# A Fourier mixing and gated FFN kernel on one core: batch 0's x ahead of the weights, half tables read mirrored, half the sines inside the thirds, batch 1's first folds on VectorE

## The chip, the core and the metric

The kernel runs on one core of a Trainium2 chip. The core has TensorE (PE; its weight loads are listed apart as PEld), VectorE (DVE), ScalarE (ACT), GpSimd (POOL), SyncE (SP), whose only work here is to issue transfers, and 16 DMA engines. The metric is the device time of one execution in microseconds, lower is better; the median over several executions is quoted.

## The reference, cut to what matters

```python
X = np.fft.fft(np.fft.fft(x, axis=1), axis=2)      # x: (8, 3008, 256), float32
x = X.real.astype(np.float32).reshape(8 * 3008, 256)
gate = 1.0 / (1.0 + np.exp(-(x @ w_gate)))         # 256 x 1536
val = x @ w_val                                    # 256 x 1536
return (gate * val @ w_out).astype(np.float32)     # 1536 x 256
```

The three weights are handed over as 8-byte floats.

## The kernel before, in words

**Sequence transform.** The transform along the 3008 positions is a product with cosine and sine tables. Symmetry cuts it: rows s, S-s, M+s and M-s (M = 1504) are folded into sums and differences, so that 756 rows remain, held as 126 partitions times 6 slots q. Frequencies are split into even ones (block 0) and odd ones (block 1), and rows by their parity (slots with even and odd q, accumulated apart in banks `ev` and `od`). The table `st` (from `stab`) holds, for cosine and sine, slot q and both blocks, 753 columns: 377 for block 0 and 376 for block 1. `half` (L500 on) makes one group of sums: `sums(*qs)` issues one product per slot, `then` copies the `ev` bank out on ScalarE, and `places` (L535 to L541) writes sums and differences of `ev` and `od` on VectorE into rows of `pk` (cosine) or `qk` (sine), 128 features by 1505 frequencies. The feature transform is folded in the same way; its middle feature (number 128) gives one row, `er`, which is handled apart: `e0_sums`, `e0_copies`, `e0_row` and `e0_spread` for batch 0, `e_fold` (L600 to L604, on POOL) and `e_sums` for the other seven batches.

**Weights.** Gate and value weights come in twelve pieces of 256 x 256 (numbers 0 to 11), the output weights in six (12 to 17). `weight_load` transfers one (512 KB), `weight_parts` (L301, L302) takes it apart on ScalarE in two operations, `weight_join` (L313 to L316) puts float32 together in three VectorE operations and one POOL addition (L318). `merge` multiplies a gate or value piece with the feature table `dt` on TensorE, and `merged` (L349) copies the result to `G`, the combined matrix of feature transform and weights. Bias values `ge` for each block of 128 hidden features come out of row 0 of `G2`: for pieces 0 to 3 by one-column products (`ge_sums`, `ge_out`), for the others by small transfers (`ge_load`, L364).

**Main loop.** 8 batches times 6 chunks of 252 frequencies times 12 blocks of 128 hidden features make 576 passes. In pass i, `front_a(i)` and `front_b(i)` multiply `G` with `pk` and `qk`; `seed` (ScalarE, L664) puts the middle feature's row times `ge` into the bank beforehand, `part` (L675) saves the state between the two; `gate_a` and `gate_b` of pass i-1 make sigmoid and products (ScalarE L689, L703; VectorE L690, L702, L706), and POOL makes sums of blocks (L712) for `back`, the product with the output weights, in a form with fewer products (its weight forms are made by `forms` on POOL, L402 to L405). For the first chunk of batch 0, `rows_start` makes plain products instead.

**Order.** Each engine's order is written out by hand (the scheduler is set to manual for PE, ScalarE, VectorE, POOL and SP): an instruction that waits holds back all behind it on its engine. Lists (`mid`, `pre`, `use`, `side`) hang further work onto passes. In pass i the order is front_a(i), gate_a(i-1), part(i), seed(i+1), gate_b(i-1), listed work, back, front_b(i), work of `side[i]`. The next batch's x is folded in `side` work: `fold_ops` gives 24 operations for batch 1, in passes 24 to 55, and `table_odd` makes a smaller table on POOL in passes 56 to 60. SP issues transfers in program order; each waits until the eighth before it has landed.

**The start before.** SP issues pieces 0 to 7, then three thirds of batch 0's x (two slots each, 1 MB) with the cosine tables of the same slots, then the sine tables, between them pieces 8 and 9, then pieces 10 to 13. TensorE runs a warm-up and pieces 0 to 7; then, third by third, folds on VectorE (`third`, `feats`; L473 to L483) and cosine sums; then the sine sums third by third with front_a of passes 0 to 2 in between; then the loop.

## Time and profile before

| | |
|---|---|
| median of 3 runs | 1929.01 us (1926.16 to 1933.58) |
| profiled execution: time, span | 1929.26 us, 1927.4 us |
| TensorE busy, of the span | 1913.6 us, 99% |
| VectorE, ScalarE, POOL busy | 1406.6, 1343.7, 1557.4 us |
| granted TensorE clock | 1.000 |
| transferred | 97.89 MB, mean 51 GB/s |

The profile lists each engine's busy time, the same in slices and stretches, groups of instructions by source line (L135 is the helper `mm`, so TensorE's groups are told apart by their tiles: `ps` weight pieces, `pe` the middle feature's sums, `ev` and `od` sequence sums, `pf` front_a with `pk` and front_b with `qk`, `po` and `rows` the output), and the chain of waits: followed back from the end, at each step what released it. A timeline row gives start, length, engine, line, operation, tiles, shapes, count, and in brackets the engine's idle time before and what ended it. One logical float32 product shows as two records.

### The profile page before, as it was taken

The numbers are of one execution on the slowest core, as the hardware profiler recorded it, in microseconds if no ns is written. First come the engines' busy times: TensorE is split into PE (matmuls) and PEld (weight loads), VectorE is DVE, ScalarE is ACT, GpSimd is POOL, SyncE is SP. The second block draws the span as 40 slices with busy tenths as digits, with TensorE's granted clock in tenths as the row PEclk, the third lists the DMA queues.
The fourth block names the chain that finished last, engine by engine and source line by source line (L and its number), as shares of the span: only waits on it lengthen the run. The fifth ranks groups of instructions, "written<-read, shape, count | busy, mean of one in ns | idle before, by whom it ended". The sixth has DMA issues, their size and how long they took to land.

```text
span 1927.4 us, 34460 instructions
## 1 busy us (share of the span) xinstructions
PE 1913.6 (99%) x11260; PEld 1787.2 (93%) x11260; DVE 1406.6 (73%) x3210; ACT 1343.7 (70%) x3147; POOL 1557.4 (81%) x2806
## 2 busy tenths in 40 slices
PE   8999999999999999999999999999999999999999
PEld 5899999999999999999999999999999999999998
DVE  7747877787767776778777777777777777766776
ACT  5777767767777677776777767777677766777775
POOL 2399989978899688986888869888788886777775
PEclk9999999999999999999999999999999999999999
DMA  9351422211121201202112121111200100011111
GB/s 302 124 100 36 107 80 53 55 38 57 20 72 30 80 14 28 80 14 80 24 43 55 20 80 23 47 49 25 80 14 15 25 17 14 15 22 20 25 17 30
DMA packets 167403, 97.89 MB, mean 51 GB/s; under 512 B 128602, under 2 KB 157372, under 8 KB 165432
## 3 DMA queue, kind: packets, MB, share of 16 engines
q1 hardware_dynamic: 166670, 95.17, 20.5%
q8 instruction: 91, 1.49, 0.3%
q14 instruction: 88, 0.72, 0.1%
q10 hardware_dynamic: 522, 0.50, 0.1%
q0 software_dynamic: 32, 0.00, 0.0%
HBM read 70.40 MB, written 47.24 MB: 61 GB/s over the span
## 4 chain that ended last, share of the span: by engine, by line
PE 93%; POOL 3%; DMA 2%; ACT 0%; DVE 0%; issue 0%; ACTq 0%; SPq 0%; POOLq 0%
PE pf L135 49%; PE po L135 40%; PE ev L135 3%; POOL sf L712 2%; DMA st<-in_stab_dram 2%; PE rows L135 1%; PE od L135 1%; DMA x<-in_xf_dram 1%; PE row L135 0%; DMA raw<-in_moe_w_val_dram 0%; POOL x L452 0%; POOL x L431 0%; POOL x L436 0%; POOL x L433 0%; PE ps L135 0%
## 5 line engine op out<-in xcount | busy, mean ns | idle before, releaser
L712 POOL TENSOR_TENSOR sf<-h 128x168 f32<-128x168 f32 (+1 forms) x935 | 516.9, 572 | 224.8 <-DVE h L706 224.1
L712 POOL TENSOR_TENSOR sf<-h,sf 128x168 f32<-128x168 f32 (+1 forms) x1122 | 614.3, 568 | 49.2 <-DVE h L706 47.8
L135 PE MATMUL pf<-pk,G 128*128 128x252 f32 (+1 forms) x2304 | 582.9, 376 | 0.5 <-ACT pf L664 0.5
L135 PE MATMUL pf<-qk,G 128*128 128x252 f32 (+1 forms) x2304 | 581.8, 375 | 1.1 <-ACT ae L675 1.1
L664 ACT ACTIVATE pf<-ek,ge 128x252 f32<-128x252 f32 (+1 forms) x1152 | 542.6, 471 | 19.3 <-DVE h L706 0.5
L706 DVE TENSOR_TENSOR h<-pf,z 128x252 f32<-128x252 f32 (+1 forms) x576 | 241.6, 419 | 417.2 <-ACT pf L703 415.5
L135 PE MATMUL po<-sf,wf 128*128 128x168 f32 (+1 forms) x2992 | 516.6, 305 | 1.4 <-POOL sf L712 1.4
L675 ACT ACTIVATE ae<-pf 128x504 f32<-128x504 f32 (+1 forms) x576 | 339.8, 590 | 249.3 <-PE pf L135 247.8
L135 PEld LDWEIGHTS pf<-pk,G 128*128 128x128 f32 x2304 | 436.9, 190 | 53.4 <-issue 1.6
L135 PEld LDWEIGHTS po<-sf,wf 128*128 128x128 f32 x2992 | 460.6, 190 | 9.9 <-POOL sf L712 1.9
L135 PE MATMUL po<-h,wf 128*128 128x168 f32 (+1 forms) x2618 | 463.4, 305 | 0.0
L135 PEld LDWEIGHTS pf<-qk,G 128*128 128x128 f32 x2304 | 410.9, 190 | 27.3 <-ACT ae L675 1.5
L690 DVE TENSOR_TENSOR z<-ae,pf 128x504 f32<-128x504 f32 (+1 forms) x576 | 386.0, 670 | 65.3 <-ACT h L689 60.7
L135 PEld LDWEIGHTS po<-h,wf 128*128 128x128 f32 x2618 | 416.6, 190 | 16.2
L830 DVE TENSOR_TENSOR c<-c 128x168 f32<-128x168 f32 (+1 forms) x929 | 424.6, 465 | 3.4
L689 ACT ACTIVATE h<-pf 128x252 f32<-128x252 f32 (+1 forms) x576 | 218.9, 380 | 205.7 <-PE pf L135 195.4
L702 DVE TENSOR_TENSOR h<-h,pf 128x252 f32<-128x252 f32 (+1 forms) x576 | 233.5, 405 | 0.0
L703 ACT ACTIVATE pf<-z 128x252 f32<-128x252 f32 (+1 forms) x576 | 211.7, 368 | 24.4 <-DVE h L702 20.8
L712 POOL TENSOR_TENSOR sf<-sf 128x168 f32<-128x168 f32 (+1 forms) x187 | 103.5, 554 | 14.7
L712 POOL TENSOR_TENSOR sf<-sf,h 128x168 f32<-128x168 f32 (+1 forms) x187 | 110.6, 592 | 0.0
L743 ACT COPY c<-po 128x504 f32<-128x504 f32 (+1 forms) x141 | 80.1, 569 | 1.1 <-PE po L135 1.1
L839 DVE STREAM_TRANSPOSE os<-c 128x256 f32<-128x256 f32 x184 | 79.9, 435 | 0.0
(152 smaller groups left out, 906.5 us busy)
## 6 DMA issues: line engine op xcount, KB each, us to landing
x<-xr SPq DMA_DIRECT2D x14, 1536.0 KB
out_dram<-os SPq DMA_DIRECT2D x368, 56.0 KB
xr<-in_xf_dram SPq DMA_DIRECT2D x14, 768.0 KB
xr<-in_xf_dram SPq DMA_DIRECT2D x35, 256.0 KB
ek<-ed SPq DMA_DIRECT2D x39, 126.0 KB
out_dram<-os SPq DMA_DIRECT2D x284, 7.0 KB
st<-in_stab_dram SPq DMA_DIRECT2D x6, 658.9 KB
x<-in_xf_dram SPq DMA_DIRECT2D x3, 1024.0 KB
```

Of the source, the lines that this page charges most:

```text
L135: nc.tensor.matmul(o, l, r, start=start, stop=stop, skip_group_check=True)
L664: nc.scalar.activation(PF[i][:, g], EK[i // NFT], AF.Copy, scale=ge[:, g, f : f + 1])
L675: nc.scalar.activation(AP[i], PF[i], AF.Copy, scale=2.0)
L689: nc.scalar.activation(H[p][:, fh, 0:n], PF[i][:, 0], AF.Sigmoid)
L690: nc.vector.tensor_tensor(z[:, :, ::-1], AP.pop(i), PF[i], op=ALU.subtract)
L702: nc.vector.tensor_tensor(h[:, fh, 0:n], h[:, fh, 0:n], pf[:, 1], op=ALU.mult)
L703: nc.scalar.activation(pf[:, 0], z[:, 0], AF.Sigmoid)
L706: nc.vector.tensor_tensor(h[:, fh, n:], pf[:, 0], z[:, 1], op=ALU.mult)
L712: nc.gpsimd.tensor_tensor(block(p, dst), block(p, a), block(p, b), op=(ALU.subtract, ALU.add)[op])
L743: (nc.vector.tensor_copy if t == 1 or t == 3 and not last else nc.scalar.copy)(C[0][:, 3 * t * R : 3 * (t + 1) * R], PO[t][:, 0 : 3 * R])
L830: engine.tensor_tensor(t[:, dst * R : (dst + 1) * R], *v, op=(ALU.subtract, ALU.add)[op])
L839: nc.vector.transpose(os_[0][:, s, 0:nb, h, :], t[:, c0 : c0 + nb * TB])
```

## The change

It touches the start and the handling of batch 1.

- SP issues the three thirds of x first, each with its cosine and sine tables, then `dt`, then pieces 0 to 9 and 12; the others follow when their buffers are free. `dt` was issued by ScalarE before.
- Only half of each table's columns is loaded (377 of 753 per slot, one transfer of 126 rows; before, 112 rows and 14 rows). The other half of the frequencies is reached by reading the table backwards (`table_of(..., True)`) with cosine and sine exchanged for odd slots, against a copy of the folded x that has its signs set (`turned`, three ScalarE operations per third, with a per-partition sign from `signs`). So each product over 377 or 376 columns becomes two of 189 or 188.
- In the thirds, TensorE makes both cosine groups and the first sine group; the second sine group follows the last third in one go. After that come the weight pieces, and front_a of passes 0 to 2 between pieces 3 to 6. Warm-up grows from 12 to 16 products.
- Pieces 0 to 3 get their bias values by `ge_load` too; the one-column products are gone.
- The middle row of batch 0 (`e0_row`) is made on POOL. For the other batches `e_fold` gets three ScalarE copies with signs.
- Ahead of the loop pieces 0 to 8 are joined and 0 to 7 multiplied; pieces 9 to 12 are joined in passes 0 to 3.
- The first eight of batch 1's fold operations run on VectorE, two in each of passes 24 to 27 (before: POOL); the other sixteen stay on POOL in passes 28 to 55, and the odd table moves two passes ahead.

```diff
-        for rows in (slice(0, 112), slice(112, NP)):
-            nc.sync.dma_start(out=ST[0][rows, t, q], in_=stab[rows, t, q])
+        nc.sync.dma_start(out=ST[0][0:NP, t, q, 0 : HE + HO], in_=stab[:, t, q, HO : NE + HO])
...
+    def weight_parts(j, which=(0, 1)):
 
         if j in RAW:
             raw, ws = RAW[j], WS[j]
             lo, hi = raw[:, :, :, 0], raw[:, :, :, 1]
-            nc.scalar.activation(ws, hi.bitcast(F32), AF.Abs)
-            nc.scalar.activation(lo, lo.bitcast(U32), AF.Copy, scale=2.0 ** -29)
+            if 0 in which:
+                nc.scalar.activation(ws, hi.bitcast(F32), AF.Abs)
+            if 1 in which:
+                nc.scalar.activation(lo, lo.bitcast(U32), AF.Copy, scale=2.0 ** -29)
...
+    def signs():
+
+        at_ = sgn.bitcast(I32)
+        nc.gpsimd.iota(at_[:, 0:1], pattern=[[0, 1]], base=0, channel_multiplier=1)
+        nc.vector.tensor_scalar(out=at_[:, 1:2], in0=at_[:, 0:1], scalar1=31, scalar2=0x3F800000 - 2 ** 31,
+                                op0=ALU.logical_shift_left, op1=ALU.bitwise_xor)
+        nc.vector.tensor_scalar(out=at_[:, 0:1], in0=at_[:, 0:1], scalar1=31, scalar2=0x3F800000,
+                                op0=ALU.logical_shift_left, op1=ALU.bitwise_xor)
+
+    def sign(q, r=False):
+
+        i = (q // 2 % 2) ^ (r and q % 2 == 0)
+        return sgn[0:NP, i : i + 1]
...
-                ops += [lambda i=i, q=q: point(pool, i, i + 1, q) for q in qs]
-                ops.append(lambda i=i: first(pool, i, i + 1, slice(0, NQ)))
+                e = nc.vector if b == 1 else pool
+                ops += [lambda i=i, q=q, e=e: point(e, i, i + 1, q) for q in qs]
+                ops.append(lambda i=i, e=e: first(e, i, i + 1, slice(0, NQ)))
...
+            def turned(q):
+                copy = lambda to, of, s: nc.scalar.activation(to, of, AF.Copy, scale=s)
+                copy(XV[:, :, q, 0:HD], x4[:, 1::-1, q, 0:HD], sign(q.start))
+                for i in range(q.start, q.stop):
+                    copy(x4[:, 3:1:-1, i, HD:D], x4[:, 3:1:-1, i, 0:HD], sign(i, True))
+            XR_[0] = [(XV[:, i], x4[:, 3 - i, :, HD:D]) for i in range(2)]
             for q in qs:
-                ops += [lambda q=q: third(q), lambda q=q: feats(q)]
+                ops += [lambda q=q: (third(q), nc.scalar.activation(
+                            XV[:, :, q, HD], x4[:, 1::-1, q, HD], AF.Copy, scale=sign(q.start))),
+                        lambda q=q: (feats(q), turned(q))]
...
+    def table_of(t, q, blk, turned=False):
+
+        if not turned:
+            return ST[0][0:NP, t, q, blk * HE : HE + blk * HO]
+        to = ST[0][0:NP, t ^ (q % 2), q]
+        return to[:, HE + HO - 1 : HE - 1 : -1] if blk else to[:, HE - 1 : 0 : -1]
+
+    def columns(blk):
+
+        return (slice(HO, NE), slice(0, HO)) if not blk else (slice(0, HO), slice(HO, NO))
...
-                mm((ev, od)[q % 2], w(q), ST[0][0:NP, int(sn), q, c0 : c0 + n], q < 2, q >= NQ - 2)
+                mm((ev, od)[q % 2][:, columns(blk)[0]], w(q), table_of(int(sn), q, blk), q < 2, q >= NQ - 2)
+            for q in sorted(qs, key=lambda q: q % 2):
+                mm((ev, od)[q % 2][:, columns(blk)[1]], XR_[0][blk][int(sn)][:, q, 0:HD],
+                   table_of(int(sn), q, blk, True), False, q >= NQ - 2)
...
-        nc.vector.memset(er[:, NK:], 0.0)
-        places(er, 0, True, od, ev)
-        places(er, 1, False, ev1, od1)
+        nc.gpsimd.memset(er[:, NK:], 0.0)
+        places(er, 0, True, od, ev, e=nc.gpsimd)
+        places(er, 1, False, ev1, od1, e=nc.gpsimd)
...
+        for q in range(0, NQ, 2):
+            nc.scalar.activation(x8[:, :, 0::2, q : q + 2], x8[:, :, 1::2, q : q + 2], AF.Copy, scale=sign(q))
...
-    nc.scalar.dma_start(out=dt, in_=dtab.rearrange("(c p) d -> p c d", p=P))
     load_x(0)
-    for j in range(8):
-        weight_load(j)
     for j in range(N3):
         load_third(j)
-        load_table(0, j)
+        for t in range(2):
+            load_table(t, j)
+    nc.sync.dma_start(out=dt, in_=dtab.rearrange("(c p) d -> p c d", p=P))
+    for j in (*range(10), 12):
+        weight_load(j)
...
-    warm(12)
-    ges = None
-    for j in range(8):
-        weight_parts(j)
-        if j > 2:
-            merged(j - 3)
-        weight_join(j, j % 3)
-        weight_use(j)
-        if j > 2 and j < 7:
-            ges = ge_sums((j - 3,), 3, ges)
-    ge_out(range(4), ges)
-    for j in (5, 6, 7):
-        merged(j)
-    for j in range(N3):
-        if j == N3 - 1:
-            weight_load(8)
-            weight_load(9)
-        load_table(1, j)
-    for j in range(10, KEEP):
-        weight_load(j)
+    signs()
+    warm(16)
     seq_start(0)
     folds = fold_ops(0, 2)
-    cos = [seq_group(0, blk, 0, (2 * blk, 2 * blk + 1)) for blk in range(2)]
+    halves = [seq_group(0, blk, 0, (2 * blk, 2 * blk + 1)) for blk in range(2)]
+    halves.append(seq_group(0, 0, 1))
     for j in range(N3):
         folds[2 * j]()
         e0_sums(j)
+        if j == N3 - 1:
+            weight_parts(0, (0,))
         folds[2 * j + 1]()
-        if j == N3 - 1:
-            e0_copies()
-            e0_row()
-        for sums, _, _ in cos:
+        for sums, _, _ in halves:
             sums(2 * j, 2 * j + 1)
-    put = [then() for _, then, _ in cos]
-    for f in put:
-        f()
-    e0_spread()
-    for i in range(N3):
-        seed(i)
-    for j in (8, 9):
-        weight_parts(j)
-        weight_join(j, NB - 1)
-    sin = [seq_group(0, blk, 1, (2 * blk, 2 * blk + 1)) for blk in range(2)]
-
-    def sines(j):
-        for sums, _, _ in sin:
-            sums(2 * j, 2 * j + 1)
-
-    for j in range(N3):
-        sines(j)
-        front_a(j)
-        if j < 2:
-            part(j)
-        if not j:
-            weight_parts(10)
-            weight_join(10, NB - 1)
-    put = [then() for _, then, _ in sin]
-    for high in range(2):
-        for f in put:
-            f(high)
-    for j in range(KEEP, len(jobs)):
-        weight_load(j)
+    weight_parts(0, (1,))
+    weight_join(0)
+    halves[0][1]()()
+    weight_parts(1)
+    halves[1][1]()()
+    weight_join(1, 2)
+    halves[2][1]()()
+    weight_parts(2)
+    halves = [seq_group(0, 1, 1, (0, 1))]
+    halves[0][0](*range(NQ))
+    e0_copies()
+    e0_row()
+
+    def piece(j):
+        merge(WS.pop(j), *jobs[j], 3 + j % 2 if j > 2 else None)
+
+    for j in range(2, 9):
+        weight_join(j, 2)
+        weight_parts(j + 1)
+        if j == 3:
+            halves[0][1]()()
+        piece(j - 2)
+        if j > 2:
+            merged(j - 3)
+            if j < 5:
+                weight_load(j + 7)
+            if j == 5:
+                weight_load(14)
+                weight_load(15)
+            if j < 7:
+                ge_load(j - 3)
+        if j == 4:
+            e0_spread()
+        if j > 4 and j < 8:
+            seed(j - 5)
+            front_a(j - 5)
+            if j < 7:
+                part(j - 5)
+    piece(7)
+    for j in (6, 7):
+        merged(j)
+    for i in (13, 16, 17):
+        weight_load(i)
     for j in range(4, 8):
         ge_load(j)
     nc.sync.dma_start(out=ed[0:1], in_=shared["er"])
-    weight_parts(11)
...
-    for j, i in ((11, 1), (12, 3), (13, 5), (14, 6), (15, 8), (16, 10), (17, 12)):
-        if j > 11:
+    for j, i in ((9, 0), (10, 1), (11, 2), (12, 3), (13, 5), (14, 6), (15, 8), (16, 10), (17, 12)):
+        if j > 9:
             pre.setdefault(i - 1, []).append(lambda j=j: weight_parts(j))
         mid.setdefault(i, []).append(lambda j=j: weight_join(j, 2))
         if jobs[j][0] == 2:
             use.setdefault(i + 2, []).append(lambda j=j: using(j))
-    for j, i in ((8, 0), (9, 1), (10, 3), (11, 4)):
+    for j, i in ((8, 1), (9, 2), (10, 3), (11, 4)):
...
-    at(4 * i0 + 5, lambda: [at(4 * i0 + i, f) for i, f in zip((8, 9, 10, 11, 12, 7), table_odd())])
+    at(4 * i0 + 5, lambda: [at(4 * i0 + i, f) for i, f in zip((6, 7, 8, 9, 10, 7), table_odd())])
...
-            slots = [i for i in slots if i < 5 * i0] + [4 * i0 + 6, 4 * i0 + 7]
+            slots = [i for i in slots if 2 * i0 + 3 < i < 5 * i0] + [4 * i0 + 6, 4 * i0 + 7]
 
         def folds(slots, b=b):
             ops = fold_ops(b + 1, 2)
+            if not b:
+                for i in range(8):
+                    at(2 * i0 + i // 2, ops[i])
+                del ops[0:8]
```

## The prediction

> **What bounds the kernel now.** I read the page first, then busy time by stretch, then the chain of waits and TensorE's waits in the start, and last ScalarE's and POOL's timelines around the second place that the change touches.
>
> ```profile
> PE 1913.6 (99%) x11260; PEld 1787.2 (93%) x11260; DVE 1406.6 (73%) x3210; ACT 1343.7 (70%) x3147; POOL 1557.4 (81%) x2806
> ```
> TensorE is busy 99% of the span of 1927.4 us: nothing can be won except where it waits. By stretch of time (busy us and instructions of TensorE, its weight loads, VectorE, ScalarE and POOL; granted clock; DMA share; GB/s):
> ```profile
> 0.00:63.00 63.00, 55.39 (x231) 38.32 (x231) 46.48 (x80) 34.07 (x66) 17.75 (x18) 1.00 0.90 277
> 63.00:167.00 104.00, 104.00 (x551) 95.28 (x552) 65.67 (x138) 79.68 (x195) 80.34 (x138) 1.00 0.35 76
> 167.00:270.00 103.00, 101.46 (x634) 93.46 (x634) 80.27 (x178) 69.64 (x164) 98.67 (x176) 1.00 0.33 73
> 8.00:14.00 6.00, 4.89 (x21) 3.61 (x21) 5.79 (x10) 5.08 (x10) 3.64 (x4) 1.00 1.05 387
> 34.00:38.00 4.00, 2.03 (x13) 0.93 (x13) 3.23 (x8) 1.49 (x4) 0.00 (x0) 1.00 1.01 225
> 36.00:38.00 2.00, 1.51 (x12) 0.79 (x5) 1.30 (x5) 1.49 (x4) 0.00 (x0) 1.00 1.01 183
> ```
> From 63 us on TensorE is full, but for 1.5 us between 167 and 270. Weight pieces come in at 387 GB/s; the stretches in which tables come in reach 225, at worst 183. The chain of waits through the start, in order of time, then what TensorE waits for in it (total, times, longest), and its one wait after it:
> ```profile
> 6.78 11.27 DMA x<-in_xf_dram
> 18.07 17.22 DMA st<-in_stab_dram
> 35.30 13.45 DMA st<-in_stab_dram
> ...
> PE ev L135 <- DMA st<-in_stab_dram: 1.7, 1, 1.7
> PE pe L135 <- DVE x L436: 1.5, 1, 1.5
> PE warm L135 <- DVE busy L878: 1.2, 1, 1.2
> PE pf L135 <- ACT ae L675: 1.1, 1, 1.1
> PE ps L135 <- POOL raw L318: 0.9, 1, 0.9
> PE pf L135 <- ACT pf L664: 0.5, 1, 0.5
> PE ev L135 <- DVE x L483: 0.5, 1, 0.5
> ...
> PE po L135 <- POOL sf L712: 1.4, 1, 1.4
> ```
> The start is a chain of transfers, and weight pieces keep TensorE busy beside it. Its useless time there is all of 8.99 us until the first piece (warm-up included), the waits of 1.7, 1.5, 1.1, 0.5 and 0.5, and 4 x 0.53 = 2.1 us of one-column bias products, which the change drops: 16.4 us in all.
>
> **The start, as changed.** Times are start to start in the rows, 0.06 us from one engine to the next. *Transfers.* Pieces 0, 1 and dt (1.31 MB) are in at 6.79 (the second piece's first reader), so the first third of x (1.05 MB) is in at 6.79 - 0.26/0.387 = 6.1; a later third takes 2.71. A half table is 126 x 2 x 377 x 4 B = 380 KB. Its rate is not in the trace: bounds 387 (0.98 us) and 183 GB/s (2.08); I take 225, the stretch with most table bytes: 1.69. Thirds land at 6.1, 12.2, 18.3, the last tables at 21.7, dt 22.3, piece 0 at 23.7, later pieces 1.36 apart. [...]
>
> *Thirds.* Folds take 2.79 us and then 1.4 (VectorE L474 to L483). New are ScalarE's signed copies, 512 and 2 x 256 elements; no row has them: plain rows give 0.57 + 2 x 0.34 = 1.25, rows with a per-partition scale (0.50 for 252) 1.65; I take 1.5. Half-width products run at half the 0.63 of the full ones. Reversed tables as moving operand are in no TensorE row; VectorE's reversed reads (1.21 for 1020) are no slower, so nothing, at most double (six mirrored halves of 0.315 in the last third: +1.9). Warm-up grows by 8 x 0.2125 to 9.6 and hides behind the first fold (8.9).
>
> *The last third.* ScalarE's first weight operation (piece 0) stands ahead of the last third's copies and waits for piece 0: 23.7 + 0.6 = 24.3, copies to 25.8. The folds were ready at 22.5, so TensorE waits 2.7. It then has 3.15: 29.0.
>
> *From there.* ScalarE: a sum's copy, piece 2's two operations, four one-row copies (0.45 + 1.15 + 1.9): 32.5. POOL now makes the middle row er (four operations of e0_row; L452's 384 columns took 1.0, so 0.9 each, 0.54 on VectorE before) between its second and third adds: second add to 33.1, row to 36.7, third add 38.0, and TensorE's third piece waits for that: 39.8, spread 40.4, its copy 40.8. Then ScalarE and TensorE alternate: per round two weight operations 1.15, G copy 0.50, seeds 1.00, wait for front_a 0.97, ae 0.52 = 4.1 us, where TensorE has only 1.73 + 0.85. Seeds end at 43.5, 47.6, 51.8. TensorE: front_a 0.85, two pieces 3.46, front_b(0): 57.0; passes 1 and 2, 1.73 + 0.85 each: 62.1; pass 3 with waits 4.3, pass 4 3.6: 70.0. Before, front_b(4) ran 66.50 to 67.35, with the same twelve pieces done. **Start: +2.6** (bounds: tables at 387 and copies at 1.25 give 65.5, -1.9; tables at 183 and copies at 1.65 give 72.5, +5.1). Covered: dt, moved from ScalarE's queue to SP's behind the tables, has its first user past 32 us; pieces 10 and 11, loaded only when the buffers of pieces 0 and 1 come free (34.5, 36.2), land before 41 and are read after 57.
>
> **e_fold.** Half tables need signed copies of the middle features too: three ScalarE operations behind four POOL ones, in pass 36. Now:
> ```profile
> 170.30 0.36 ACT L703 ACTIVATE pf<-z 128x252 f32<-128x252 f32 x1
> 171.23 0.38 ACT L689 ACTIVATE h<-pf 128x252 f32<-128x252 f32 x1 [0.57 <-PE pf L135]
> 172.02 0.59 ACT L675 ACTIVATE ae<-pf 128x504 f32<-128x504 f32 x1 [0.41 <-PE pf L135]
> ...
> 171.26 1.54 POOL L712 TENSOR_TENSOR sf<-h,sf 128x168 f32<-128x168 f32 x3 [0.40 <-DVE h L706]
> ...
> 175.19 0.28 POOL L604 TENSOR_TENSOR x<-x 126x42 f32<-126x42 f32 x1
> ```
> The copies stand between L703 (ended 170.66) and the next L689 on ScalarE. POOL, held by its six sums, finishes e_fold at 175.47. Copies of 28 elements at 0.2 (nearest row: 2x1, 0.20): 176.1; L689 starts there instead of 171.23, ae ends at 177.0, and front_b(37), which started at 173.25, starts at 177.05: **+3.8**, on a full TensorE. Bounds: 3.3 (copies nearly free) and 4.9 (ScalarE's whole delay).
>
> **Batch 1's folds.** Six POOL operations of 1.32 and two of 0.22 (L423, L427: 8.3 us) become VectorE operations in passes 24 to 27. L474's 1.21 for 1020 gives 0.68 for 510: 6 x 0.68 + 2 x 0.16 = 4.4 us in 12.5. VectorE was busy 4.3 and 4.7 of 10 there: covered. In front of them waits batch 1's x, issued at 120.97 and 3.15 MB long (8.1 us), before a place on VectorE at 133.6; were it later, the gate products behind would wait with it. POOL gains little: it was idle at 171 and 211 all the same, so the 257.77 wait comes of work after 211. There one group of feature operations (1.6) moves out, and the odd table's ends (0.8) move in front: **-0.8**, at best -1.4, at worst 0.
>
> **Sum.** 1927.4 + 2.6 + 3.8 - 0.8 = 1933.0 span; the profiled run took 1929.26, 1.86 more than its span, so 1934.9, say **1935**. That run is 0.25 above the median of 1929.01.
>
> **Rivals.**
> 1. *The tables land as fast as weights.* For: 387 GB/s with 2 KB rows. Against: every table stretch is slower. 1929.3 - 1.9 + 3.8 - 0.8 = 1930.4.
> 2. *Clearly slower, by the bias values.* The first biases (ge) now come through DMA, in order behind weight loads on SP, not through TensorE; the seeds wait for them. I took 2.9 us from G copy to landing, hidden behind the 4.1 us rounds. The page has one small DMA with a time, zero<-nil, 5.2 us; with 0.7 for issue that is 5.9, and the third seed ends at 54.4, +2.6: 1937.5. It decides from about 4 us more: at 8.9 us the start costs +11.2 and the time is 1943.5. For: weight pieces lie ahead in the same queue. Against: the biases are one word per partition.
> 3. *All waits of the start gone.* TensorE cannot start useful work before 6.1 + 2.79 = 8.9, so of the 16.4 us at most 7.5 can go, and the 1.4 at 257: 1929.3 - 8.9 = 1920.4, and that without any wait in the new start and at e_fold. Even this is within half a per cent.
>
> **How the numbers follow.** Half a per cent (9.6 us) is about what a measurement here tells from no change. Forecast 0.52 (1935), rival 1 and what lies towards rival 3 0.23, rival 2 or tables beyond 183 GB/s 0.22; 0.03 is left for a gain that I do not see, since even rival 3 falls short of one. The bound of slower is 1929.0 + 9.6 = 1938.7, so same 0.75, slower 0.22, faster 0.03. The range leaves out 2 in 10: 1929.5 (rival 1 and POOL's best case, less a little) to 1941 (tables at 183 GB/s and the late biases together: 1929.3 + 5.1 + 2.6 + 3.8).
>
> **What would show it.** Right: x third 2 folded near 21 us; a wait of over 2 us on ScalarE for piece 0 ahead of the last signed copies; TensorE waiting 0.9 to 1.6 for seeds three times between 42 and 52; front_b(4) ending near 70; a ScalarE wait of 4 to 5 us on POOL L654 and a TensorE wait near 3.8 in pass 37; no VectorE wait on x in passes 24 to 27; the later wait near 0.6. Wrong: front_b(4) before 67, no wait at e_fold (POOL done before its sums), seeds waiting on ge, or TensorE waits in passes 24 to 30.

## The result, and the profile after

The changed kernel takes **1938.39 us** (median of six runs, 1936.24 to 1939.21) against 1928.37 us (median of six, 1926.16 to 1933.58): a ratio of the runs of **1.0046** (of the two medians alone 1.0052), 95% interval 1.0036 to 1.0057. The interval lies wholly above 1: the changed kernel is slower, by about half a per cent. The profiled execution took 1936.24 us with a span of 1934.4 us; it is the shortest of the six, so the span's 7.0 us over before is less than the median's 10.0.

The profile after, busy time of the whole span and then by stretch (from:to, length, busy us and instructions of TensorE, its weight loads, VectorE, ScalarE and POOL; granted TensorE clock, DMA share, GB/s):
```profile
PE 1916.6 (99%) x11348; PEld 1796.2 (93%) x11348; DVE 1408.1 (73%) x3215; ACT 1347.4 (70%) x3161; POOL 1553.7 (80%) x2804
```
```profile
0.00:63.00 63.00, 54.05 (x286) 43.84 (x286) 41.83 (x73) 35.23 (x72) 18.76 (x23) 1.00 0.76 242
63.00:167.00 104.00, 103.66 (x544) 94.40 (x544) 71.98 (x146) 80.44 (x197) 76.96 (x131) 1.00 0.35 76
167.00:270.00 103.00, 98.95 (x590) 90.88 (x588) 74.55 (x168) 69.99 (x165) 91.79 (x166) 0.98 0.29 73
```
The third line holds the news: TensorE is busy 98.95 of 103 us where it was busy 101.46, and its granted clock is 0.98 where it was 1.00. What TensorE waits for up to 270 us (total, times, longest):
```profile
PE pf L135 <- ACT ae L730: 3.8, 2, 3.6
PE pf L135 <- ACT pf L719: 3.7, 4, 1.4
PE ps L135 <- POOL raw L327: 1.9, 2, 1.7
PE ev L135 <- ACT st L510: 1.5, 1, 1.5
...
PE ps L135 <- ACT ek L644: 0.6, 1, 0.6
PE po L135 <- POOL sf L767: 0.2, 1, 0.2
```
Gone are the waits for tables in the start, the one of the middle feature's sums for x (1.5), and the 1.40 us at 257.77; the 0.2 behind POOL's sums stands three passes before that place, at 255.33. New are one of 3.6 us, and in the start waits for ScalarE's signed copies (st), POOL's third add (raw) and the seeds (pf). The long one, in the timelines of POOL, ScalarE and TensorE (start, us busy, what; in brackets the wait ahead of it and what ended it):
```profile
177.68 0.28 POOL L654 TENSOR_TENSOR x<-x 126x42 f32<-126x42 f32 x1
```
```profile
178.00 0.74 ACT L656 ACTIVATE x<-x,sgn 126x28 f32<-126x28 f32 x3 [4.83 <-POOL x L654]
178.64 0.36 ACT L744 ACTIVATE h<-pf 128x252 f32<-128x252 f32 x1
178.90 0.57 ACT L730 ACTIVATE ae<-pf 128x504 f32<-128x504 f32 x1
```
```profile
179.52 2.05 PE L135 MATMUL pf<-qk,G 128*128 128x252 f32 x4 [3.61 <-ACT ae L730]
181.37 1.76 PE L135 MATMUL pf<-pk,G 128*128 128x252 f32 x4
182.97 1.59 PE L135 MATMUL po<-h,wf 128*128 128x168 f32 x10
184.39 1.01 PE L135 MATMUL pf<-qk,G 128*128 128x252 f32 x4
```
The pause is the forecast one: ScalarE's signed copies (L656) stand 4.83 us behind e_fold on POOL, and ae, on which front_b(37) waits, comes that much later. But the four products behind the pause take 2.05 us, where the same four take 1.01 at 184.39. By stretch around it, the granted clock (third number from the end) says why:
```profile
176.00:179.40 3.40, 0.00 (x0) 0.00 (x0) 0.37 (x1) 1.41 (x6) 3.24 (x8) 1.00 0.00 0
179.60:182.80 3.20, 3.20 (x8) 2.62 (x9) 2.33 (x7) 1.39 (x4) 1.85 (x3) 0.50 0.07 19
183.00:186.00 3.00, 3.00 (x19) 2.84 (x18) 0.60 (x3) 2.62 (x6) 0.54 (x2) 1.00 0.26 65
```
An idle stretch of 3.4 us is followed by one at half clock (the clock's own record: 0.5 from 179.46 for 3.41 us), and the clock is full again behind it. Before had no such record ahead of its end.

The sum by the starts of front_b: front_b(4) starts 2.51 us later than before (69.01 against 66.50); from front_b(36) to front_b(38) it takes 11.76 instead of 6.25, 5.51 more, of which 3.76 are the pause and 1.75 the half clock; from front_b(38) to front_b(570) 1719.60 instead of 1720.40, 0.80 less; the rest 0.2 less. 2.51 + 5.51 - 0.80 - 0.2 = 7.0, the whole difference of the spans.

The last third in the start, ScalarE and then TensorE:
```profile
23.11 0.66 ACT L309 ACTIVATE raw<-raw 128x512 f32<-128x512 f32 x1 [2.11 <-DMA raw<-in_moe_w_gate_dram]
23.67 0.71 ACT L510 ACTIVATE st<-x,sgn 126x512 f32<-126x512 f32 x1
24.29 0.89 ACT L510 ACTIVATE x<-x,sgn 126x256 f32<-126x256 f32 x2
```
```profile
24.43 0.59 PE L135 MATMUL ev<-st 126*128 126x188 f32 x2 [1.50 <-ACT st L510]
```
ScalarE stands 2.11 us in front of weight piece 0, the copies behind it, and TensorE 1.50 us behind the copies.

### The profile page after: what moved, and what is told of

Same layout as the page of the kernel before. It is cut to its first block, busy times and chain, and to the rows that moved or that the text cites. A ratio compares the mean times of both kernels' runs of the same rounds, so it can differ in the third digit from the quotient of the medians.

```text
span 1934.4 us, 34673 instructions
## 1 busy us (share of the span) xinstructions
PE 1916.6 (99%) x11348; PEld 1796.2 (93%) x11348; DVE 1408.1 (73%) x3215; ACT 1347.4 (70%) x3161; POOL 1553.7 (80%) x2804
## 3 DMA queue, kind: packets, MB, share of 16 engines
q8 instruction: 91, 1.49, 0.3%
## 4 chain that ended last, share of the span: by engine, by line
PE 96%; ACT 1%; DMA 1%; SPq 1%; POOL 1%; issue 0%; DVE 0%; ACTq 0%; POOLq 0%
PE pf L135 50%; PE po L135 41%; PE ev L135 3%; PE rows L135 1%; PE od L135 1%; DMA raw<-in_moe_w_gate_dram 1%; POOL sf L767 0%; SPq L206 0%; PE row L135 0%; PE ps L135 0%; ACT pf L719 0%; DMA raw<-in_moe_w_val_dram 0%; ACT G L358 0%; SPq L155 0%; PE pe L135 0%
## 5 line engine op out<-in xcount | busy, mean ns | idle before, releaser
L758 ACT ACTIVATE pf<-z 128x252 f32<-128x252 f32 (+1 forms) x576 | 211.7, 367 | 23.5 <-DVE h L757 19.9
```

The lines of the kernel that those rows point to most:

```text
L758: nc.scalar.activation(pf[:, 0], z[:, 0], AF.Sigmoid)
```

## The experiments

Three theories were put against each other first. *A*: the wait of e_fold's copies costs its pause, and the pause itself the half clock behind it, 5.5 us in all; the rest is the start. *Rivals*: the clock fell for another reason (B), or the loss lies elsewhere and only shows there (C). The kernel before ran beside each experiment, and its median was not the same each time (1928.37 to 1930.51 us); so the ratio to it says more than a difference between the medians of two experiments.

### 1. The copies two passes later

```diff
+    def e_signs():
         for q in range(0, NQ, 2):
             nc.scalar.activation(x8[:, :, 0::2, q : q + 2], ...)
...
     at(3 * i0, e_fold)
+    at(3 * i0 + 2, e_signs)
```


> The changed kernel with the three signed copies of the middle features issued two passes later (end of pass 38) than the four POOL operations they wait for; nothing else differs. Theory A (the copies, standing in ScalarE's queue behind POOL, cost the 3.61 us pause of TensorE, and the pause itself halves the clock for the 3.41 us behind it): no TensorE wait over 0.5 us and no 0.5 clock record near 180 us, span 1934.4 - 3.7 - 1.7 = 1929.0, time near 1930.9. Rival B (the pause costs 3.7, the clock fell for another reason): span 1930.7, a clock record of 0.5 still there at some place. Rival C (the loss lies elsewhere, the pause is only seen there): time within 1 us of the changed kernel's 1936.2 to 1939.2.

Measured: 1933.31 us (nine runs, 1932.74 to 1933.83), before beside it 1929.61, ratio 1.0021 (1.0012 to 1.0030): under the changed kernel by 5.1 us in the medians and by 4.8 in the two ratios, but 2.4 above the 1930.9 of theory A. front_b(36) to front_b(38) takes 6.25 us, to the hundredth what it took before the change; the copies run at 182.12 and nobody waits. So A holds at this place. The 2.4 lie in the start, where front_b(4) begins at 71.31, 2.3 later than in the changed kernel's profile. The clock's record has a half-clock stretch there, where none was expected (TensorE's timeline, then the stretch):
```profile
23.29 0.49 PE L135 MATMUL pe<-st 126*1 126x188 f32 x4 [1.26 <-DMA st<-in_stab_dram]
...
26.26 0.59 PE L135 MATMUL ev<-st 126*128 126x188 f32 x2 [1.65 <-ACT st L510]
```
```profile
27.00:30.00 3.00, 3.00 (x12) 3.00 (x11) 1.79 (x5) 2.55 (x6) 1.30 (x1) 0.50 1.05 406
```
Here the last sine table came late as well (1.26), and the wait for the copies (1.65) was followed by half clock from 26.86 for 3.41 us. That is what B asked for in form ("still there at some place"), and the second experiment tells whether the pause makes it.

### 2. The copies alone, on the kernel before

```diff
         tt(x8[:, :, 3], x8[:, :, 0], x8[:, :, 2], op=ALU.subtract)
+        for q in range(0, NQ, 2):
+            nc.scalar.activation(x8[:, :, 0::2, q : q + 2], x8[:, :, 1::2, q : q + 2], AF.Copy, scale=-1.0)
```


> The kernel before with one thing added: the same three ScalarE copies behind e_fold's four POOL operations, scale -1, into the two slots of x8 that are dead by then (the output does not depend on them). Theory A: ScalarE waits 4 to 5 us on POOL in pass 36, TensorE 3.3 to 3.8 us in pass 37, then a clock record of 0.5 of 3.4 us: span 1927.4 + 3.7 + 1.7 = 1932.8, time near 1934.7. Rival B: wait as in A, no clock record, time near 1933.0. Rival C: the wait needs the changed start or the moved folds to come about, time within 1 us of before.

Measured: 1934.87 us (six runs, 1932.19 to 1937.94) against 1929.61, ratio 1.0033 (1.0022 to 1.0044): 5.3 us more in the medians, 6.4 by the ratio. ScalarE, TensorE and the stretch behind the pause:
```profile
177.12 0.46 ACT L606 ACTIVATE x<-x 126x28 f32<-126x28 f32 x3 [4.82 <-POOL x L604]
```
```profile
178.38 1.71 PE L135 MATMUL pf<-qk,G 128*128 128x252 f32 x4 [3.32 <-ACT ae L677]
```
```profile
49.20:52.40 3.20, 3.20 (x6) 1.68 (x5) 1.77 (x3) 2.05 (x4) 1.02 (x1) 0.50 0.38 142
178.90:182.10 3.20, 3.20 (x9) 2.63 (x9) 2.11 (x5) 1.28 (x4) 1.67 (x3) 0.50 0.15 25
```
Three small ScalarE operations, put into a kernel whose TensorE was full there, make the pause and the half clock, and front_b(36) to front_b(38) takes 11.52 instead of 6.25, 5.27 more: A, with B and C out. The first stretch is the same thing in the start of the kernel before: in this execution TensorE waited 2.98 us for a sine table (1.67 in the profile before, with the clock full) and ran at half clock behind it.

### 3. The folds on VectorE alone, on the kernel before

```diff
-                ops += [lambda i=i, q=q: point(pool, i, i + 1, q) for q in qs]
-                ops.append(lambda i=i: first(pool, i, i + 1, slice(0, NQ)))
+                e = nc.vector if b == 1 else pool
+                ops += [lambda i=i, q=q, e=e: point(e, i, i + 1, q) for q in qs]
+                ops.append(lambda i=i, e=e: first(e, i, i + 1, slice(0, NQ)))
...
+            if not b:
+                for i in range(8):
+                    at(2 * i0 + i // 2, ops[i])
+                del ops[0:8]
```
(with the slots of the other folds and of the odd table as in the change)

> The kernel before with only batch 1's first eight folds on VectorE (passes 24 to 27), with the slots and the odd table's slots as in the change. The prediction's step: covered on VectorE, the wait of 1.40 us at 257.77 falls by 0.8 (to 1.4): time 0.8 to 1.4 under before, ratio 0.9993 to 0.9996. Rival: gate products queue behind the folds on VectorE and TensorE waits in passes 24 to 28: 0 to +2 us, waits there in the trace.

Measured: 1927.04 us (twelve runs, 1925.64 to 1932.87) against 1929.61, ratio 0.9990 (0.9981 to 1.0000). Run again beside experiment 9:

> The same edit as e3_folds_alone (the kernel before with only batch 1's first eight folds on VectorE), beside e9 on one chip, since it is the one version measured under the kernel before. If the 1.40 us wait is all that it takes away: 1.4 under before, ratio 0.9993; if the first measurement's 0.999 was the start's transfers, ratio 0.9995 to 1.0005.

Measured: 1927.35 us (eleven runs) against 1928.54, ratio 0.9992 (0.9983 to 1.0002). In the trace of the first the wait of 1.40 us is gone, one of 0.2 has come up three passes earlier, and none stands in passes 24 to 28; front_b(38) to front_b(570) takes 1719.53, 0.87 less than before. So this part is a gain of some 0.9 us, as the step had it, and at the edge of what these runs can show.

### 4. The middle row on VectorE again

```diff
-        nc.gpsimd.memset(er[:, NK:], 0.0)
-        places(er, 0, True, od, ev, e=nc.gpsimd)
-        places(er, 1, False, ev1, od1, e=nc.gpsimd)
+        nc.vector.memset(er[:, NK:], 0.0)
+        places(er, 0, True, od, ev)
+        places(er, 1, False, ev1, od1)
```


> The changed kernel with batch 0's middle row er made on VectorE again, as before the change, so that POOL goes from the second piece's add to the third's. If the row on POOL sets the end of the start: TensorE's waits of 1.70 (third piece, on POOL) and 0.55 (fourth, behind the spread) go, ScalarE's 3.57 us wait for ek too, the seeds come some 2.5 us earlier and front_b(4) starts near 66.7 instead of 69.0; time 2 to 2.5 under the changed kernel, the pause in pass 37 unchanged. Rival: ScalarE's rounds or VectorE's joins, now 2.2 us later, take its place, and front_b(4) moves by less than 1 us.

Measured: 1938.20 us (five runs, 1936.36 to 1941.48), no different from the changed kernel. The profiled execution cannot decide why: TensorE waited 1.44 for a table and 1.66 for the copies, ran at half clock for 6.83 us from 25.52, and so came so late to the third piece that it waited only 0.54 there. Experiment 1, with the row on POOL, waited 0.48 there after its own half clock. A gain of 2 to 2.5 us does not show in the median; how much of the 1.70 us the row would cost in an undisturbed start stays open.

### 5 to 7. Three edits of the start, each on top of experiment 1

Piece 0's first operation behind the signed copies:
```diff
-        if j == N3 - 1:
-            weight_parts(0, (0,))
         folds[2 * j + 1]()
...
-    weight_parts(0, (1,))
+    weight_parts(0)
```


> On top of e1_signs_later: ScalarE's first operation on weight piece 0 is issued behind the last third's signed copies instead of ahead of them; nothing else differs. Theory (the copies wait in ScalarE's queue for piece 0, TensorE waits 1.65 us for the copies, and this wait is what makes the 3.41 us at half clock at 26.9 us): TensorE's wait on st is gone, since the folds are done at 22.5 and copies need 1.5; no clock record of 0.5 in the start; time 1933.3 - 1.65 - 1.7 = 1930.0. Rival (the weight pieces and POOL's adds set what comes behind): the wait moves to the third piece, the time falls by less than 1.

Tables cut as before the change:
```diff
-        nc.sync.dma_start(out=ST[0][0:NP, t, q, 0 : HE + HO], in_=stab[:, t, q, HO : NE + HO])
+        for rows in (slice(0, 112), slice(112, NP)):
+            nc.sync.dma_start(out=ST[0][rows, t, q, 0 : HE + HO], in_=stab[rows, t, q, HO : NE + HO])
```


> On top of e1_signs_later: each table transfer is cut in 112 and 14 rows again, as before the change; nothing else differs. [...]

ae a round later than its seeds:
```diff
         if j > 4 and j < 8:
+            if j > 5:
+                part(j - 6)
             seed(j - 5)
             front_a(j - 5)
-            if j < 7:
-                part(j - 5)
```


> On top of e1_signs_later: in the start's last rounds ScalarE's ae operation comes one round later, behind the next round's weight operations and G copy, so that ScalarE does not wait for the front_a products; nothing else differs. Theory (ScalarE's rounds of 4.1 to 4.3 us, of which 1.2 are this wait, set the seeds and TensorE's waits of 1.44 and 1.42): rounds of 3.1, the two waits fall to 0.2 to 0.5 each, time 1933.3 - 1.9 = 1931.4. Rival (VectorE's joins or the landing of ge set the rounds): rounds stay over 3.8, time 1933.3.

Measured, eleven runs each, before beside them 1928.43: piece 0 later **1931.97** (ratio 1.0018, 1.0009 to 1.0026), tables cut **1931.69** (1.0016, 1.0008 to 1.0025), ae later **1929.92** (1.0002, 0.9993 to 1.0010). TensorE's longest waits in the start of the three, from the lists of waits in this order:
```profile
PE ps L135 <- POOL raw L327: 2.5, 2, 2.4
```
```profile
PE ev L135 <- ACT st L511: 2.3, 1, 2.3
```
```profile
PE ev L135 <- ACT st L510: 1.9, 1, 1.9
...
PE pf L135 <- ACT pf L721: 0.9, 2, 0.5
```
With piece 0 later the wait for the copies is gone and the third piece's has grown from 0.5 to 2.4: the rival's answer, a wait moved. The median is 1.3 lower than in experiment 1, but the intervals of the two ratios overlap.

The tables cut came near 1932, the author's estimate ahead of the run. It had the six tables land 1.4 us earlier in all than in experiment 1, and piece 0 behind them at 23.5 instead of 24.9; no trace shows that 1.4. TensorE no longer waits for the last table (1.26 in experiment 1), but waits 2.3 instead of 1.65 for the copies, which stand behind piece 0; that landed at 23.8. TensorE's waits up to front_b(4), without its first for the warm-up, sum to 8.0 us in experiment 1, to 8.2 with piece 0 later, to 8.7 with the tables cut and to 5.2 with ae later. So the first two edits took no waiting away; the 1.4 and 1.6 us by which their front_b(4) came earlier are no more than the 1.7 that the half-clock stretch cost experiment 1 (half of its 3.41, an estimate), and neither of their traces has one in the start.

The waits for the last table tell more than the time: in the four executions with 126 rows in one transfer and the changed kernel's order (experiments 1, 4, 5, 7) TensorE waited 1.26, 1.44, 1.21 and 0.73 us for it, in the changed kernel's own not at all, and in the four with the cut (experiments 6, 8, 9 and 11) never. The traces list when each transfer's landing is counted on its semaphore: 14 counts for each table of 126 rows, 16 for each part of 112 (in the changed kernel's trace the last table's 14 lie between 20.49 and 21.42 us). What one count stands for was not shown, and the waits do not follow from their number: thirteen of the last table's fourteen counts were in by 21.3 to 21.9 us in all five executions; the fourteenth came at 21.4 in the changed kernel's own and at 22.4 to 23.6 in the four that waited. With the cut all counts were in by 20.2 to 21.3. Why one count lags stays open.

With ae later the seeds come every 3.0 us instead of 4.3 (ScalarE's timeline):
```profile
43.15 1.00 ACT L721 ACTIVATE pf<-ek,ge 128x252 f32<-128x252 f32 x2
46.16 0.97 ACT L721 ACTIVATE pf<-ek,ge 128x252 f32<-128x252 f32 x2
49.14 0.98 ACT L721 ACTIVATE pf<-ek,ge 128x252 f32<-128x252 f32 x2
```
The waits of 1.44 and 1.42 are gone, and the median falls by 3.4 us against experiment 1, more than the 2.9 of these waits and more than the 1.9 expected. So of the three edits only this one took waiting out of the start: ScalarE's rounds were the largest part of what it could give back.

### 8. All of it together

Experiment 1, the three edits of 5 to 7 and the row on VectorE.

> The changed kernel with all of these at once: signed copies two passes later, piece 0's first operation behind the last signed copies, tables cut in 112 and 14, ae one round later, the middle row on VectorE. If the waits seen are the whole loss and nothing new takes their place: start at 69.0 - 1.65 - 1.9 - 1.7 (third piece) = 63.8 or a little more for front_b(4), no half clock anywhere, time 1933.3 - 1.7 (half clock) - 1.65 - 1.9 - 1.0 = 1927, under the kernel before by 2 to 3. Rival (the transfers set the start: last table 22.7, piece 0 at 24): 1929 to 1931, no better than before.

Measured: 1930.05 us (eleven runs) against 1928.43, ratio 1.0008 (0.9999 to 1.0017). The expected 1927 was missed. One long wait is left in the start (from the list of waits, then the stretch behind it):
```profile
PE ps L135 <- POOL raw L328: 3.2, 2, 3.0
```
```profile
38.50:45.00 6.50, 5.95 (x14) 3.82 (x14) 6.12 (x10) 3.29 (x7) 3.85 (x3) 0.50 0.65 209
```
VectorE's row (2.3 us) stands ahead of its third join, so the third piece's add comes late; one pause of 3.0 us, and half clock for 6.83 us, which costs about another 3.4 (half of it, an estimate). A new wait took the place of the old ones, and the clock doubled its price. The time lies in the rival's 1929 to 1931, but not by the rival's way: in this trace nothing waits for a table or for piece 0.

### 9 and 11. The row dealt out, the spread behind the fourth piece

On top of experiment 8, first:
```diff
-        nc.vector.memset(er[:, NK:], 0.0)
-        places(er, 0, True, od, ev)
-        places(er, 1, False, ev1, od1)
+        nc.gpsimd.memset(er[:, NK:], 0.0)
+        return [lambda h=h, a=a: places(er, *a, h, nc.gpsimd)
+                for a in ((0, True, od, ev), (1, False, ev1, od1)) for h in range(2)]
...
-    e0_row()
+    row = e0_row()
+    row.pop(0)()
...
     for j in range(2, 9):
+        if 2 < j < 5:
+            row.pop(0)()
+            if j == 4:
+                row.pop(0)()
         weight_join(j, 2)
...
+        if j == 5:
+            e0_spread()
         piece(j - 2)
...
-        if j == 4:
-            e0_spread()
         if j > 4 and j < 8:
-            if j > 5:
-                part(j - 6)
             seed(j - 5)
-            front_a(j - 5)
+        if j > 5:
+            front_a(j - 6)
+        if j > 6:
+            part(j - 7)
```


> On top of e8_all_mended: the middle row is made on POOL again, but its four operations are dealt out, one or two between the adds of pieces 1 to 4, so that neither VectorE's third join nor POOL's third add stands behind the whole row; the spread comes one round later, front_a and ae of the start's rounds one round later than the seeds. Theory (in e8 VectorE's row ahead of the third join made the 3.00 us wait and, through it, 6.8 us at half clock): the third piece waits under 0.6, no clock record of 0.5, later waits of 1 to 1.4 for VectorE's joins (2.2 us a piece against TensorE's 1.73) remain: time 1930.0 - 1.5 = 1928.5. Rival (VectorE's joins bind all the way and the 3.00 us only spread over several pieces): TensorE's waits in the start sum to the same 5 us, time 1929.3 to 1930 without the half clock.

Measured: 1927.88 us (eleven runs, 1926.22 to 1928.57) against 1928.54, ratio 0.9988 (0.9978 to 0.9997). TensorE's waits up to front_b(4), without its first for the warm-up, sum to 4.0 us instead of 5.5, so they did not only spread; but a half-clock stretch of 3.41 us is still there, from 39.36, behind 1.55 us idle in the 3.41 us ahead of it, one step of the clock's record. The waits that made it:
```profile
PE ek L135 <- POOL er L585: 1.1, 1, 1.1
...
PE ps L135 <- ACT ek L645: 0.5, 1, 0.5
```
So last, the spread behind the fourth piece's products, and the two banks of the pieces swapped (`4 - j % 2` for `3 + j % 2`):

> On top of e9_row_spread: the row's spread (and its ScalarE copy) is issued behind the fourth piece's products instead of ahead of them, and the two banks that the pieces take in turn are swapped, so that the fourth piece does not wait for the copy; nothing else differs. Theory (in e9 the waits of 1.14 for the row and 0.46 for its copy, 1.55 us idle in one gate window, made the 3.41 us at half clock): the fourth piece starts at 37.5 where the spread stood, TensorE's waits from 35 to 43 us sum to under 1.2, no clock record of 0.5, time 1927.9 - 1.7 - 0.5 = 1925.7. Rival (the half clock is not tied to these waits): a clock record of 0.5 stays, time within 0.6 of 1927.9.

Measured: **1926.54 us** (eleven runs, 1925.44 to 1927.34) against 1930.51, ratio **0.9981** (0.9972 to 0.9990). The fourth piece starts at 36.95, TensorE's waits from 35 to 43 us sum to 0.9, its granted clock was 1.0 in ten of the eleven runs, and no half clock is in its record ahead of the end. The first stretch of its profile, and TensorE's longest waits up to 300 us:
```profile
0.00:63.00 63.00, 58.73 (x305) 47.71 (x306) 46.45 (x81) 39.87 (x82) 20.36 (x24) 1.00 0.75 243
```
```profile
PE warm L135 <- DVE busy L936: 1.2, 1, 1.2
PE ps L135 <- POOL raw L328: 0.7, 1, 0.7
PE ps L135 <- ACT ek L645: 0.6, 1, 0.6
PE pf L135 <- ACT pf L722: 0.5, 1, 0.5
```
TensorE is busy 58.73 of the first 63 us, where the changed kernel had 54.05 and the kernel before 55.39; front_b(4) starts at 64.09. Of the versions measured this has the lowest median, and its interval and that of experiment 9 alone lie wholly under 1. Three things make the gain smaller than it looks. The kernel before was slow beside it (1930.51, where it was 1928.4 to 1929.6 beside the others), so the gain may be 0.1% rather than 0.2%. The folds on VectorE bring 0.8 us of it. And the new start is steadier more than it is faster: the kernel before took 1925.85 to 1934.14 us in 97 runs, this version 1925.44 to 1927.34 in eleven, while in the best start of before on record (the execution of experiment 3) front_b(4) began at 63.80, earlier than here.

## Why the prediction was right, and where it was not

The forecast was 1935 in a range of 1929.5 to 1941, with 0.75 for no change that can be told. The time fell in the range, 3.4 above the forecast; the ratio's interval, 0.36 to 0.57 per cent, lies across the half per cent from which the prediction would call a change slower.

**e_fold, +3.8: the mechanism right, the term mis-sized.** ScalarE's wait on POOL L654 (forecast 4 to 5 us, measured 4.83) and TensorE's in pass 37 (forecast 3.8, measured 3.61) came as worked out. The term should have been 5.5: it priced the pause and not the half clock behind it, 1.75 us. Its upper bound of 4.9 had no room for that either. Experiment 2 shows the whole price with these three operations alone (+5.3), experiment 1 its disappearance without them (5.1).

**The start, +2.6: met in the profiled execution (2.51), but by luck.** The thirds of x were first used at 6.32, 11.94 and 17.78 (forecast 6.1, 12.2, 18.3), piece 0 at 23.11 (23.7), and the copies took 1.5 us as taken. But TensorE waited 1.50 in the last third, not 2.7: piece 0 was 0.6 earlier, and the first mirrored products need only the first of the copies, not all of them. Mirrored tables as moving operand cost nothing more (0.32 for 188 columns in either direction), as taken. POOL's row held the third piece as forecast (a wait of 1.70). ScalarE was 1.4 ahead of the forecast behind the one-row copies, the third seed 0.9, front_b(0) 0.6. Then the lead was lost: ScalarE's rounds took 4.3 instead of 4.1, and from the end of front_b(0) to that of front_b(4) 13.6 passed instead of 13.0. The three waits for seeds at 42 to 52 us (forecast 0.9 to 1.6) measured 0.43, 1.45 and 1.42.

These errors cancelled, and other executions of the same two starts would have given another difference. The start before began front_b(4) at 66.50 in its profile, and at 63.80, 68.15 and 68.16 in those of experiments 3, 2 and 10, which leave it unchanged. In the changed kernel's profile piece 0 had landed by 23.1; in those of experiments 1, 4, 5 and 7, whose transfers are the same, it landed at 24.2 to 25.3, and the last table was late in all four. By the medians the start cost more than 2.6: experiment 1, free of the pause, still lies 3.7 above the kernel before; with the folds' 0.8 and the rest's 0.2 added back, that is 4.7 us for the start (an estimate). So this term too is mis-sized for the usual execution.

**Batch 1's folds, -0.8: the number right, the way to it not.** -0.80 in the changed kernel, -0.87 alone; no TensorE wait came up in passes 24 to 30. But the wait of 1.40 did not shrink to 0.6. It is gone, which brings front_b(63) forward by 1.5; and three passes earlier, at front_b(60), TensorE now loses 0.9 behind POOL's sums (0.8 in experiment 3):
```profile
255.33 1.24 PE L135 MATMUL po<-sf,wf 128*128 128x168 f32 x4 [0.18 <-POOL sf L767]
```
Four such products take 0.73 us elsewhere. The odd table, which now stands two passes earlier on POOL, is a likely reason; no run moves it alone.

**The rivals.** Tables as fast as weights (1930.4): no; the last table was in time in the profiled execution, but piece 0 behind the tables landed only 0.6 earlier than forecast. The bias values by DMA (1937.5 to 1943.5): no; the seeds waited for the middle row and ScalarE's rounds, never for ge. The time came near that rival's lower figure by another way. All waits of the start gone (1920.4): far from it; the new start had 7.8 us of waits up to front_b(4), without the first for the warm-up.

**The median, 1935: its last step failed.** The profiled run of before was close to the median of its runs, and the sum took that over. The changed kernel's profiled run is the shortest of six; the others ran at a granted clock of 0.997 to 0.999, and their spans are up to 3.0 us longer. What happened in those executions no trace shows; the late transfers named above and the half clock behind them are a likely cause, not a shown one. The executions of experiments 1, 4 and 7, whose start is the changed kernel's but for what each edits (7 only in the later rounds), show half clock behind the waits of the last third, 3.4 to 6.8 us long, at a cost of about half that, 1.7 to 3.4 (an estimate from pass 37 of the changed kernel, where 3.41 us at half clock cost 1.75), which is the size of the difference.

## What to carry to other kernels

Where TensorE is busy 99% of the time, a pause can cost more than its length: where more than some 1.5 us of idle time fell into one 3.41 us step of the clock (last section), a step at half clock followed in these traces, 1.75 us more in pass 37, or an estimated 3.4 where a second one came. A small operation can hold up all that is queued behind it on its engine: the three signed copies, 0.74 us of work, stood 4.83 us on ScalarE behind POOL's e_fold, and ae behind them, so that TensorE stood 3.61 us. Put such an operation into the queue when its input is there (two passes later cost nothing here, and gave back 5.1 us). And when one wait of a start is removed, look at once for the next: of the edits of the start two only moved waits, one took some away, and only all of them with the row dealt out beat the kernel before. Where a start hangs on transfers, one profiled execution of each kernel is not enough to size it: the same start differed by 4.4 us between executions.

## What was not expected of the hardware

In these traces the granted clock of TensorE goes down to 0.5 and up to 1.0 in steps on a grid. In each trace the borders of the clock records, but for the last end, are whole multiples of 3.413 us apart (in the changed kernel's from 5.38 to 1933.91, 565 steps; in experiment 2 from 49.06 to 178.76, 38 steps; in experiment 4 from 25.52 to 182.53, 46 steps), and the phase of the grid differs from execution to execution: counted from the start of the span, the borders lie 1.97, 1.27 and 1.63 us past a multiple of 3.413 in these three. TensorE's idle time summed in each step at full clock, from 5 us to the last 20 us of the program, in all 13 traces:

```
idle in a step of 3.41 us            clock in the next step
3.41 (changed kernel, pass 37)       0.5
3.03, 2.99 (experiment 2)            0.5
2.72, 1.95 (experiment 4)            0.5
2.54 (experiment 8)                  0.5
2.36 (experiment 10)                 0.5
2.09 (experiment 7)                  0.5
1.65 (experiment 1)                  0.5
1.55 (experiment 9)                  0.5
1.50 (changed kernel, last third)    1.0
1.49 (before; experiment 6)          1.0
all others, 1.45 and less            1.0
```

So what a pause cost went by where it fell on the grid: the 2.30 us wait of experiment 6 was cut by a border into 0.81 and 1.49, and the clock stayed full; the 1.65 us wait of experiment 1 lay in one step, and a step at half clock followed. Up to the last 20 us of the program, the least idle time in a step that half clock followed is 1.55 us (experiment 9), the most that full clock followed 1.50 (the changed kernel's last third). Two things stay open. In those last 20 us, in traces of the experiments, steps with 1.77 and 1.89 us idle were followed by full clock, so idle time alone is not the rule; what the products of a step count for was not tried. And a step at half clock was sometimes followed by another (experiment 4 with 1.15 and 0.87 us idle in it, experiment 8 with 0.20), without a limit that fits all.

The kernel before has this too: its spread from 1926 to 1934 us goes at least partly back to its wait for a sine table, 1.67 us in its profile, 2.98 and 2.36 us in experiments 2 and 10, whose start is the same, with a half-clock step behind the two longer ones; in experiment 3, again with the same start, the wait was 0.47 us, and that is the execution with the best start.
